# A convolution's intermediate values stored with another index first, and elementwise work moved from GpSimd to VectorE and ScalarE

## The chip, the cores and the metric

The kernel runs on one core of a Trainium2 chip. In the profile's names the core's engines are PE (TensorE: matrix products, with its weight loads as PEld), DVE (VectorE), ACT (ScalarE), POOL (GpSimd) and SP (SyncE, which here only issues DMAs). The metric is the device time of one execution in microseconds (us), given as the median of several runs.

## What is computed

Two layers of the same pair of blocks work on 2048 tokens of 512 channels, all in float32. The first block of a pair normalizes each token, convolves every channel along the tokens with a filter as long as the sequence, and adds the result. The second scores all tokens, sends the best two through a gated feed-forward network, and adds what comes out to those two tokens.

```python
P = exp((A * dt[:, None])[:, :, None] * pos)          # A: 512 x 128 complex, pos: 0..2047
K = 2.0 * einsum("dn,dnl->dl", C, P).real              # one filter per channel
y = irfft(rfft(u, 2 * L) * rfft(K, 2 * L))[..., :L]    # u: normalized x, by channel
x = x + (y + u * D_skip)
h = layernorm(x); r = h @ w_r; idx = argsort(-r)[:2]   # two tokens
x = x + h;  x[idx] += sigmoid(r[idx]) * ((silu(h[idx] @ w_gate) * (h[idx] @ w_up)) @ w_down)
```

The same filters serve both layers.

## The kernel before

The 512 channels are worked on in four blocks (`c` = 0 to 3) of 128. A block of x lies in a tile of 128 partitions with 16 tokens each. Each convolution is a transform in two steps, a product and the inverse in two steps, all made of small matrix products:

- `load`, `norm`: the block is loaded into `z`, and `affine` applies scale and shift, one of 16 slices at a time. Strings name the engine of each slice (A: ACT, G: POOL, V: DVE): in the second layer `NORM2` for blocks 1 to 3, `NORM0` for block 0.
- `f1a`, `f1b` (L815, L819): a product on PE, then a transpose on DVE, in eight parts, give the tile `g`, ordered by the first transform index.
- Then eight groups (`gi`). In the first layer's blocks 0 to 2: `kf_load`, `front_mm`, `front_tt` (p, L790), `back_mm` (pv, L801). In block 3 of the first layer and in all of the second: `group_kf` loads the filter's transform `kf` from DRAM, `group_mm` makes `pu` (L739), `group_tt` multiplies it with `kf` into `p` (DVE, L828, two buffers), and `group_y` forms the four parts of `y` (L843 a difference, L841 a sum; two buffers), each from one half of the partitions. They run on POOL, but for the last two groups of block 3, where the second half (`par` = 1) is DVE's. `i1_mm` turns `y` into `pv` (L849).
- `v_cp` (L1043) copies `pv` from PSUM on ACT. For blocks 0 to 2 the copy is a small tile `w` (two buffers), and `v_st` (L1046) stores it to DRAM in `vds`; once all eight are there, four loads (`v_ld`, `fin_load`, L872) bring the block back as `v` with another index on the partitions. `quad_mm` (po, L878) takes the last step on PE in four quarters, each with `d4`, and `quad_add` (L1058) adds it to x. Block 3 uses transposes on DVE (L860) in place of the trip through DRAM.
- Statistics and dot products for the next block follow on DVE (and a product on POOL), and `store` writes x. In the second layer `scale` applies the routed stage's normalization to x, one of 16 slices at a time, by the string `SCALE2`.

The DRAM tile `vds` has the shape 128 x 32 x 128: the partition of `pv` first (quarter g and 32 values b), then the 32 values k of the first transform index, then the channels. A store writes 2 KB for each partition. A load takes one quarter g: 32 partitions, one for each k, and for each of them 32 pieces of 512 bytes, so each load fills its 32 partitions for all b, and every quarter of po needs all four loads.

Beside the first layer's blocks 0 to 2, all engines also make the filters, in 32 steps (`KStep`: integer phases and decays on POOL, sines on ACT, products on DVE, contraction and transform on PE). The second layer has none of that.

The order of all this is written out by hand: the dictionary `PLAN` gives each operation of a lane (`t_y`, `t_vld`, ...) its place in one of five agendas: the first layer up to block 3; block 3 (`e_`); the routed stage (`r1`); the second layer (`t_`); the last routed stage (`r2`). `run` sorts an agenda and issues it, and `in_order` keeps each engine, SP's queue of DMAs included, in that order. An instruction that waits holds up all that stands behind it on its engine.

Of the kernel before, what the change touches and what calls it, by code (L numbers as in the profile page):

```python
# [32 lines left out]
    first=[7, 25],  # L33
    dt=[0, 1, 2, 3, 4, 5, 8, 10, 11, 12, 16, 18, 20, 24, 26, 27, 45, 51],
    setup=[
# [3 lines left out]
    ],  # L39
    setup2=[  # L40
# [3 lines left out]
    ],  # L44
    table=[191, 192, 193, 196, 197, 204, 205, 212, 220, 221, 223, 236, 237, 238, 239, 240, 243, 244, 246, 252, 253, 258, 259, 290],
    w=[101],
    x0=[21, 34, 91, 172],
    stat0=[
# [3 lines left out]
    ],  # L52
    params=[462, 484, 732, 784, 933, 1213],
    z=[261, 539, 841, 1189],
    norm=[
# [3 lines left out]
    ],  # L59
    f1a=[  # L60
        353, 402, 428, 451, 467, 490, 499, 521, 751, 772, 786, 788, 805, 812, 827, 839, 1004, 1087, 1097, 1102, 1121, 1126, 1136,
        1144, 1379, 1419, 1431, 1447, 1457, 1466, 1490, 1496,
    ],
    f1b=[
        370, 406, 446, 454, 472, 493, 519, 572, 766, 779, 787, 795, 806, 822, 831, 961, 1074, 1095, 1098, 1116, 1124, 1134, 1139,
        1166, 1409, 1423, 1436, 1449, 1465, 1475, 1493, 1524,
    ],
    kf_mm=[525, 530, 538, 560, 564, 566, 575, 579, 873, 901, 916, 918, 928, 929, 949, 950, 1207, 1218, 1226, 1227, 1245, 1252, 1253, 1273],
    kf_cp=[526, 548, 550, 561, 573, 574, 580, 585, 881, 902, 917, 926, 943, 946, 958, 973, 1219, 1223, 1231, 1232, 1251, 1254, 1268, 1276],
    kf_st=[553, 563, 594, 602, 934, 940, 966, 980, 1242, 1257, 1265, 1277],  # L70
    kf_load=[
        593, 615, 619, 649, 691, 692, 705, 748, 971, 981, 1005, 1006, 1007, 1048, 1062, 1079, 1263, 1288, 1305, 1325, 1341, 1369,
        1376, 1382,
    ],
    front_mm=[
        590, 604, 638, 661, 679, 702, 721, 749, 969, 991, 1008, 1026, 1034, 1055, 1063, 1069, 1286, 1306, 1324, 1336, 1340, 1363,
        1384, 1408,
    ],
    front_tt=[
        597, 624, 650, 674, 696, 708, 734, 758, 986, 996, 1018, 1032, 1045, 1057, 1065, 1085, 1299, 1307, 1328, 1337, 1349, 1371,  # L80
        1394, 1422,
    ],
# [28 lines left out]
    phase=[
# [7 lines left out]
    ],  # L119
    decay=[  # L120
# [9 lines left out]
    ],  # L130
    trig=[
# [5 lines left out]
    ],  # L137
    prod_b=[
# [238 lines left out]
def build(tc, x, lar, aim, cr, ci, ldt, dsk, wr, wg, wu, wd, d1_h, d1k_h, d4_h, w2_h, w3_h, w3b_h, sm_h, out):  # L377
# [6 lines left out]
    with ctx, in_order(tc, ORDER):  # L384
# [4 lines left out]
        def st(shape, nm, dt=F32, bufs=1):  # L389
            return cp.tile(shape, dt, name=nm, tag=nm, bufs=bufs)  # L390
# [1326 lines left out]
```

## Time and profile before

| | |
|---|---|
| median of 3 runs | 648.99 us (648.71 to 652.69) |
| the profiled execution | 647.57 us, span 645.7 us |
| mean granted clock of PE | 0.941 |
| HBM traffic | 82.82 MB read, 39.07 MB written |
| DMA packets | 83580, mean 190 GB/s |
| stores of w to `vds` | 48 of 256 KB, 4.0 us median to landing |
| loads of v from `vds` | 24 of 512 KB, 9.0 us median to landing |
| y on POOL | 152 of 160, some 0.73 us each |

The page gives the busy time of each engine with its share of the span. Busy time is no verdict on its own: an engine that is busy 70% of the span can be the bound in one stage and idle in another. Rows of groups read: line, engine, operation, output and inputs, count, then busy time and the mean of one in ns, then idle time just before and what ended it. Rows of waits read: who waited for whom, total us, times, and the longest. Rows of the timeline and of the chain begin with start and duration in us.

### The profile page before, as it was taken

Reading aid. Unit: us, or ns where it says so; the run is one execution under the profiler, and the core shown is the slowest. Engines: PE = TensorE matmul, PEld = TensorE weight load, DVE = VectorE, ACT = ScalarE, POOL = GpSimd, SP = SyncE. Lnnn points to the kernel's source line nnn. Section 1 sums busy time; section 2 is a strip of 40 time slices with the busy share of each in tenths; the row PEclk is TensorE's granted clock in tenths of the full one; section 3 lists DMA queues with packets and bytes.
Section 4 is the critical chain, followed back from the end, with each engine's and each line's share of the span. In section 5 each row is a group of like instructions: output and inputs, shape, how many; then the busy total and the mean of one; then the engine's idle time right before and its main releaser. Section 6 shows DMA issues by size and latency. Waiting matters only on the chain.

```text
span 645.7 us, 14016 instructions
## 1 busy us (share of the span) xinstructions
PE 459.8 (71%) x5316; PEld 348.4 (54%) x5316; DVE 461.7 (72%) x1004; ACT 326.2 (51%) x621; POOL 407.0 (63%) x630
## 2 busy tenths in 40 slices
PE   1002346778977689886986888777997998868846
PEld 0002334568864578656874675524786766664612
DVE  6997798757788656886886748735775679549941
ACT  3265847687957644678564323123365142142291
POOL 2489879788968334677362184360299889896280
PEclk9999986899999899999998999968999999889958
DMA  8736045887776768797758379964788999793962
GB/s 198 221 84 132 1 181 187 308 256 211 204 161 123 243 187 240 144 202 230 224 143 132 88 207 305 322 220 88 167 206 228 238 250 260 187 206 91 269 193 69
DMA packets 83580, 122.81 MB, mean 190 GB/s; under 512 B 6036, under 2 KB 61240, under 8 KB 79032
## 3 DMA queue, kind: packets, MB, share of 16 engines
q1 hardware_dynamic: 83384, 121.89, 71.2%
q8 instruction: 42, 0.69, 0.5%
q14 instruction: 26, 0.21, 0.1%
q0 software_dynamic: 128, 0.02, 0.0%
HBM read 82.82 MB, written 39.07 MB: 189 GB/s over the span
## 4 chain that ended last, share of the span: by engine, by line
DVE 22%; DMA 22%; PE 22%; POOL 14%; ACT 8%; issue 7%; SPq 4%; POOLq 0%; DVEq 0%; ACTq 0%
DMA kf<-kfd 4%; POOL y L843 4%; POOL y L841 4%; DMA kfd<-kd 4%; PE zf L815 4%; PE pv L801 4%; DMA v<-vd 4%; DMA vd<-w 3%; DVE sc L698 2%; DVE g L819 2%; PE po L878 2%; PE pv L849 2%; DMA b<-xs,b 2%; PE pg L1367 2%; DMA wgu<-in_wu 1%
## 5 line engine op out<-in xcount | busy, mean ns | idle before, releaser
L655 POOL TENSOR_TENSOR ph<-ph,pi 128x32 int32<-128x32 int32 (+4 forms) x160 | 88.0, 552 | 61.0 <-ACT ph L649 47.5
L667 POOL TENSOR_TENSOR mg<-mg,pf 128x32 f32<-128x32 f32 (+4 forms) x160 | 91.9, 574 | 32.1 <-ACT mg L660 25.3
L706 PE MATMUL pk<-sc 128*32 128x64 f32 x2048 | 39.6, 235 | 61.1 <-DVE rq0a L913 36.0
L698 DVE TENSOR_TENSOR sc<-tr,mg 128x1024 f32<-128x1024 f32 x64 | 76.8, 1209 | 5.3 <-ACT tr L683 3.6
L815 PE MATMUL zf<-z,d 128*128 128x256 f32 x256 | 74.6, 425 | 8.3 <-DVE g L819 5.3
L819 DVE STREAM_TRANSPOSE g<-zf 128x512 f32<-128x512 f32 x64 | 66.7, 1063 | 17.5 <-PE zf L815 16.3
L843 POOL TENSOR_TENSOR y<-p 64x256 f32<-64x256 f32 x76 | 55.2, 726 | 34.1 <-DVE p L828 27.4
L706 PEld LDWEIGHTS pk<-sc 128*32 128x32 f32 x2048 | 34.2, 120 | 72.0 <-ACT rq0b L911 36.3
L1043 ACT ACTIVATE w<-pv 128x512 f32<-128x512 f32 x48 | 28.4, 594 | 75.6 <-PE pv L849 26.8
L849 PE MATMUL pv<-y,w 128*128 128x128 f32 x320 | 51.4, 298 | 15.3 <-POOL y L841 15.1
L815 PEld LDWEIGHTS zf<-z,d 128*128 128x128 f32 x256 | 48.0, 205 | 23.5 <-DVE g L819 10.6
L828 DVE TENSOR_TENSOR p<-pu,kf 128x1024 f32<-128x1024 f32 x32 | 38.9, 1218 | 29.3 <-POOL y L841 21.3
L841 POOL TENSOR_TENSOR y<-p 64x256 f32<-64x256 f32 x76 | 55.1, 725 | 4.8
L849 PEld LDWEIGHTS pv<-y,w 128*128 128x128 f32 x320 | 42.4, 198 | 26.8 <-POOL y L841 21.3
L720 PE MATMUL kq<-d1k,kt 128*64 128x128 f32 x512 | 40.9, 309 | 22.4 <-DVE kt L713 20.7
L720 PEld LDWEIGHTS kq<-d1k,kt 128*64 128x64 f32 x512 | 32.1, 154 | 31.9 <-DVE kt L713 21.3
L730 ACT ACTIVATE gk<-kq 128x512 f32<-128x512 f32 x32 | 34.0, 1062 | 24.9 <-PE kq L720 23.4
L790 DVE TENSOR_TENSOR p<-pu,kf 128x1024 f32<-128x1024 f32 x24 | 29.2, 1218 | 22.7 <-DMA kf<-kfd 13.7
L739 PE MATMUL pu<-g,w 128*64 128x128 f32 x640 | 44.1, 287 | 1.5 <-DVE p L828 1.2
L739 PEld LDWEIGHTS pu<-g,w 128*64 128x64 f32 x640 | 36.9, 143 | 9.5 <-DVE p L828 3.5
L801 PE MATMUL pv<-p,w 128*128 128x128 f32 x192 | 38.4, 282 | 3.7 <-ACT w L1043 2.6
L801 PE MATMUL pv<-p,w3b 128*128 128x128 f32 x192 | 37.1, 275 | 0.0
(347 smaller groups left out, 1064.8 us busy)
## 6 DMA issues: line engine op xcount, KB each, us to landing
kf<-kfd SPq DMA_DIRECT2D x144, 128.0 KB, 3.7
vd<-w SPq DMA_DIRECT2D x48, 256.0 KB, 4.0
v<-vd SPq DMA_DIRECT2D x24, 512.0 KB, 9.0
kfd<-kd SPq DMA_DIRECT2D x16, 512.0 KB, 4.2
wd<-in_wd SPq DMA_DIRECT2D x4, 1792.0 KB, 17.1
x<-in_x SPq DMA_DIRECT2D x8, 512.0 KB, 7.0
w<-in_w SPq DMA_DIRECT2D x2, 2048.0 KB, 8.3
z<-in_x SPq DMA_DIRECT2D x8, 512.0 KB, 6.8
```

The costliest lines, as they stand in the source:

```text
L655: G.tensor_tensor(self.ph[:, :, n : 2 * n], self.ph[:, :, 0:n], self.step_of(self.pis, k + 1, n), op=OP.add)
L667: G.tensor_tensor(mg[:, :, 0:2, n : 2 * n], mg[:, :, 0:2, 0:n], by, op=OP.mult)
L698: V.tensor_tensor(sc.rearrange("p d (t i) -> p d t i", t=3)[:, :, 0:3:2, :], t, self.mg[:, :, 0:3:2, :], op=OP.mult)
L706: T.matmul(self.pk[32 * g : 32 * g + 32, e, :], t[:, 0:32], t[:, 32:96], start=k == 1, stop=k == 0, tile_position=(0, 32 * g))
L720: T.matmul(self.pq[64 * ri : 64 * ri + 64, e].rearrange("p g k -> p (g k)"), self.kt[:, e].rearrange("p h b -> p (h b)"), d1k[:, 128 * ri ...
L739: T.matmul(pt[64 * par : 64 * par + 64, ri, q, :], w2[:, k1, 64 * ri : 64 * ri + 64], src[:, k1, :], start=True, stop=True, tile_position= ...
L801: T.matmul(pv[:, k, :], w[:, j, :], p[t][:, k % 2, k // 2, :], start=t == 0, stop=t == 1)
L815: T.matmul(pf[:, 16 * s : 16 * s + 16, :], d1[:, 128 * s : 128 * s + 128], z[:, :, 16 * q : 16 * q + 16], start=True, stop=True)
L819: V.transpose(g[:, :, 16 * q : 16 * q + 16].rearrange("p k e -> p e k"), pf.rearrange("p b e -> p e b"))
L841: E.tensor_tensor(y[64:128, :, par, :], p[1][ls, 0], p[0][ls, 1], op=OP.add)
L843: E.tensor_tensor(y[0:64, :, par, :], p[0][ls, 0], p[1][ls, 1], op=OP.subtract)
L849: T.matmul(pv[:, k, :], w3[:, 4 * gi + k, :], y[:, k // 2, k % 2, :], start=True, stop=True)
```

## The change

It has three edits and a new order.

The DRAM tile `vds` becomes 32 x 128 x 128: k first, then the 128 partitions of `pv`, then channels. A store now writes, for each partition, four pieces of 512 bytes. A load takes eight values b of all 32 k and all four quarters g, with (k, g) as one index over the 128 partitions, and each partition receives one run of 4 KB. Loads 0 and 1 bring all that the first two quarters of po need, loads 2 and 3 the rest. Since the partitions of `v` are in another order now, `d4` gets a second copy with its rows permuted to match, used by `quad_mm`; `fin_mm` keeps the first.

In the second layer's blocks 0 to 2, one of the four parts of y in each group (the sum with `par` = 1) goes from POOL to DVE: 24 in all. `NORM2` and `SCALE2` become all A.

All lanes of `PLAN` are drawn anew; two of them stand below for their shape.

```diff
-    t_vld=[206, 215, 225, 230, 327, 328, 362, 364, 477, 481, 503, 508],
-    t_qm=[255, 271, 278, 303, 395, 431, 441, 448, 537, 539, 556, 561],
+    t_vld=[224, 228, 246, 280, 351, 367, 376, 430, 486, 491, 492, 499],
+    t_qm=[256, 259, 302, 323, 385, 389, 456, 461, 510, 526, 531, 558],
...
-NORM2 = "AAAAAAVAAAGGAAGA"
-SCALE2 = "VAAAAGAAAAAGAAAA"
+NORM2 = "AAAAAAAAAAAAAAAA"
+SCALE2 = "AAAAAAAAAAAAAAAA"
...
-        d4=d4.reshape(128, 64).astype(f),
+        d4=np.stack([d4.reshape(128, 64), d4.reshape(4, 32, 64).transpose(1, 0, 2).reshape(128, 64)], 1).astype(f),
...
-        d4 = st([128, 64], "d4")
+        d4 = st([128, 2, 64], "d4")
...
-        vds = [[dr.tile([128, 32, CH], F32, name=f"vd{i}_{c}", tag=f"vd{i}_{c}") for c in range(3)] for i in range(2)]
+        vds = [[dr.tile([32, 128, CH], F32, name=f"vd{i}_{c}", tag=f"vd{i}_{c}") for c in range(3)] for i in range(2)]
...
-            E = V if c == 3 and gi >= 6 and par else G
+            E = V if par and (c == 3 and gi >= 6 or c < 3 and layer and add) else G
...
-                T.matmul(po[64 * s : 64 * s + 64], d4, vt[:, 16 * s : 16 * s + 16, :], start=False, stop=True, tile_position=(0, 64 * s))
+                T.matmul(po[64 * s : 64 * s + 64], d4[:, 0], vt[:, 16 * s : 16 * s + 16, :], start=False, stop=True, tile_position=(0, 64 * s))
...
-            nc.sync.dma_start(vt[32 * g : 32 * g + 32], vds[layer][c][32 * g : 32 * g + 32].rearrange("b k e -> k b e"))
+            b0 = 16 * (g % 2) + 8 * (g // 2)
+            src = vds[layer][c].rearrange("k (g b) e -> (k g) b e", g=4)[:, b0 : b0 + 8, :]
+            nc.sync.dma_start(vt[:, b0 : b0 + 8, :], src)
...
-                T.matmul(po[64 * s : 64 * s + 64], d4, vt[:, b0 : b0 + 4, :], start=True, stop=True, tile_position=(0, 64 * s))
+                T.matmul(po[64 * s : 64 * s + 64], d4[:, 1], vt[:, b0 : b0 + 4, :], start=True, stop=True, tile_position=(0, 64 * s))
...
-                nc.sync.dma_start(vds[self.layer][self.c][:, 4 * i : 4 * i + 4, :], self.y.pop(("w", i)))
+                nc.sync.dma_start(vds[self.layer][self.c][4 * i : 4 * i + 4].rearrange("k p e -> p k e"), self.y.pop(("w", i)))
```

More of the change, by code (lines that the diff above doesn't have):

```diff
@@ L32 @@
 PLAN = dict(
-    first=[7, 25],
-    dt=[0, 1, 2, 3, 4, 5, 8, 10, 11, 12, 16, 18, 20, 24, 26, 27, 45, 51],
+    first=[11, 29],
+    dt=[0, 1, 2, 3, 5, 6, 7, 9, 10, 16, 18, 19, 20, 25, 26, 27, 35, 45],
     setup=[
[3 rows of a table removed]
[3 rows of a table added]
     ],
     setup2=[
[3 rows of a table removed]
-    ],
-    table=[191, 192, 193, 196, 197, 204, 205, 212, 220, 221, 223, 236, 237, 238, 239, 240, 243, 244, 246, 252, 253, 258, 259, 290],
-    w=[101],
-    x0=[21, 34, 91, 172],
[3 rows of a table added]
+    ],
+    table=[183, 204, 208, 209, 210, 211, 215, 223, 226, 229, 230, 235, 239, 240, 241, 242, 243, 245, 246, 252, 257, 260, 261, 267],
@@ L48 @@
+    w=[218],
+    x0=[17, 21, 113, 176],
     stat0=[
[3 rows of a table removed]
-    ],
-    params=[462, 484, 732, 784, 933, 1213],
-    z=[261, 539, 841, 1189],
[3 rows of a table added]
+    ],
+    params=[467, 525, 720, 782, 934, 1200],
+    z=[262, 559, 864, 1172],
     norm=[
[3 rows of a table removed]
[3 rows of a table added]
     ],
     f1a=[
-        353, 402, 428, 451, 467, 490, 499, 521, 751, 772, 786, 788, 805, 812, 827, 839, 1004, 1087, 1097, 1102, 1121, 1126, 1136,
-        1144, 1379, 1419, 1431, 1447, 1457, 1466, 1490, 1496,
+        357, 390, 443, 455, 472, 480, 491, 528, 752, 764, 771, 788, 801, 818, 829, 851, 1021, 1090, 1099, 1107, 1118, 1133, 1146,
+        1149, 1399, 1410, 1420, 1434, 1465, 1473, 1488, 1498,
@@ L77 @@
-        1384, 1408,
+        609, 617, 635, 658, 673, 708, 733, 749, 955, 996, 1018, 1024, 1043, 1062, 1070, 1075, 1277, 1287, 1305, 1324, 1346, 1365,
+        1374, 1405,
     ],
     front_tt=[
-        597, 624, 650, 674, 696, 708, 734, 758, 986, 996, 1018, 1032, 1045, 1057, 1065, 1085, 1299, 1307, 1328, 1337, 1349, 1371,
-        1394, 1422,
+        612, 631, 649, 668, 693, 723, 743, 760, 974, 999, 1020, 1035, 1045, 1063, 1072, 1082, 1283, 1303, 1314, 1336, 1355, 1367,
+        1384, 1411,
@@ L101 @@
+        1539, 1540, 1542, 1544, 1545,
     ],
-    store=[941, 1222, 1528],
+    store=[944, 1208, 1524],
     phase_0=[
-        137, 151, 218, 312, 329, 373, 392, 431, 473, 495, 522, 557, 598, 622, 663, 706, 738, 778, 843, 851, 911, 983, 1038, 1078,
-        1120, 1156, 1183, 1225, 1267, 1347, 1387, 1437,
+        136, 153, 202, 280, 335, 372, 398, 441, 469, 490, 524, 553, 582, 626, 664, 699, 765, 785, 822, 856, 921, 973, 1033, 1086,
+        1105, 1164, 1191, 1230, 1281, 1323, 1364, 1406,
     ],
@@ new lines @@
+    e_kmm=[1, 2, 4, 8, 12, 27, 28, 51],
+    e_kcp=[3, 5, 7, 10, 24, 36, 53, 63],
+    e_kst=[105, 119, 131, 164],
+    e_mm=[6, 11, 21, 22, 35, 45, 46, 60],
+    e_tt=[9, 15, 23, 29, 44, 56, 57, 74],
+    e_y=[14, 16, 17, 18, 19, 20, 25, 26, 32, 34, 37, 38, 39, 40, 41, 42, 48, 50, 52, 55, 59, 61, 65, 68, 69, 70, 72, 76, 78, 79, 80, 82],
+    e_i1=[30, 31, 47, 49, 64, 73, 77, 83],
+    e_v=[33, 43, 58, 62, 71, 75, 81, 84],
+    e_f0=[87, 67, 66, 54, 97, 88, 86, 117],
+    e_ft=[85, 89, 94, 96, 99, 106, 108, 114],
@@ L178 @@
+    e_fm=[90, 93, 95, 101, 102, 107, 121, 125],
+    e_fb=[98, 100, 103, 104, 115, 116, 123, 129],
+    e_w=[13, 91, 122, 134, 147, 149, 152, 160],
+    e_hm=[120, 127, 137, 156],
     e_hs=[
-        111, 115, 116, 129, 131, 132, 135, 136, 137, 138, 139, 140, 141, 145, 146, 147, 148, 149, 151, 153, 154, 155, 156, 157, 159,
-        160, 161, 162, 163, 164, 165, 167,
-    ],
-    e_hd=[123, 125, 158, 166],
-    e_st=[127],
+        109, 110, 111, 112, 118, 124, 126, 132, 133, 136, 138, 139, 140, 141, 142, 143, 144, 145, 146, 148, 150, 151, 153, 154, 155,
+        157, 158, 159, 161, 162, 163, 165,
+    ],
@@ L199 @@
+    r1_tab=[53, 59, 67, 71, 74, 81, 87, 99, 100],
+    r1_chg=[33, 69, 72, 75, 76, 83, 93, 94, 95, 96, 102, 103, 104, 105, 106, 137, 139, 141, 146],
+    r1_z=[47],
+    r1_n=[114, 115, 116, 117, 119, 120, 121, 122, 123, 124, 125, 126, 128, 129, 132, 133],
+    r1_fa=[142, 145, 150, 155, 160, 165, 168, 169],
+    r1_fb=[144, 147, 156, 162, 163, 166, 174, 175],
+    t_patch=[1, 2, 3, 4, 5, 6, 10, 20],
+    t_kf=[7, 8, 9, 17, 71, 105, 168, 210, 225, 282, 315, 348, 364, 388, 466, 478],
     t_mm=[
-        32, 37, 44, 45, 63, 98, 109, 123, 144, 156, 166, 181, 190, 218, 245, 251, 280, 287, 302, 316, 334, 361, 367, 401, 421, 427,
@@ L243 @@
+    t_f1a=[49, 50, 55, 64, 90, 97, 98, 112, 203, 204, 208, 213, 227, 232, 251, 252, 326, 330, 347, 352, 358, 363, 373, 391],
+    t_f1b=[51, 54, 85, 89, 94, 107, 117, 118, 205, 207, 216, 223, 237, 239, 260, 261, 335, 336, 354, 356, 366, 382, 405, 406],
+    t_f0=[546, 553, 560, 569, 577, 586, 581, 556],
+    t_hm=[585, 590, 642, 653],
     t_hs=[
-        580, 584, 589, 595, 601, 607, 608, 609, 610, 613, 614, 618, 621, 623, 624, 625, 629, 630, 635, 636, 638, 642, 643, 644, 645,
-        646, 648, 651, 652, 653, 654, 655,
+        579, 580, 583, 587, 588, 593, 594, 597, 602, 603, 605, 613, 615, 618, 623, 625, 626, 627, 628, 630, 631, 634, 636, 637, 638,
+        639, 640, 643, 646, 650, 656, 657,
@@ L282 @@
-    r2_w=[0, 1, 5, 6, 7, 8, 9, 10, 11, 12, 13, 14, 15, 16, 18, 19, 20, 21, 24, 25, 26, 27, 28, 29, 30, 31, 33, 55],
+        656, 659, 717, 742, 744, 756, 798, 809, 1008, 1022, 1064, 1065, 1080, 1081, 1097, 1108, 1317, 1331, 1350, 1379, 1380, 1425,
+        1441, 1442,
+    ],
+    v_ld=[814, 815, 816, 854, 1111, 1121, 1126, 1127, 1461, 1467, 1483, 1494],
+    quad_mm=[849, 852, 874, 886, 1162, 1173, 1187, 1192, 1490, 1499, 1504, 1521],
+    quad_add=[850, 855, 883, 887, 1163, 1182, 1188, 1196, 1495, 1502, 1509, 1522],
@@ new lines @@
+    t_vst=[93, 95, 111, 128, 144, 150, 195, 196, 221, 222, 238, 254, 265, 300, 311, 340, 350, 371, 372, 380, 403, 422, 444, 460],
+    t_vld=[224, 228, 246, 280, 351, 367, 376, 430, 486, 491, 492, 499],
+    t_qm=[256, 259, 302, 323, 385, 389, 456, 461, 510, 526, 531, 558],
+    t_qa=[262, 293, 319, 383, 395, 445, 504, 517, 527, 528, 541, 563],
+    t_dm=[287, 359, 412, 413, 452, 470, 518, 522, 559, 582, 596, 629],
+    t_ds=[337, 379, 424, 459, 501, 521, 534, 548, 567, 595, 619, 648],
+    t_ft=[554, 555, 565, 572, 573, 592, 600, 601],
@@ L283 @@
+    t_fm=[557, 561, 568, 575, 584, 599, 608, 617],
+    t_fb=[564, 566, 574, 576, 589, 607, 616, 621],
+    e_wd=[92, 113],
+    t_wd=[570, 571],
+    r1_w=[0, 1, 2, 3, 4, 5, 6, 7, 8, 9, 10, 11, 12, 13, 15, 22, 23, 24, 29, 31, 34, 40, 49, 73, 78, 79, 84, 118],
+    r2_w=[0, 1, 2, 3, 4, 5, 6, 7, 8, 9, 10, 11, 12, 13, 14, 15, 16, 18, 19, 31, 42, 45, 47, 51, 53, 54, 55, 57],
 )
```

140 lines of the change are left out of this document (50 added, 90 removed), and 109 rows, old and new, of tables (decay, norm, out, phase).

## The prediction

> **What bounds the kernel now.** I read the page's shares, its slices and the chain that ended last, cut the span into stages with the table of windows, and asked for waits and groups inside the stage that the change touches most.
>
> ```profile
> PE 459.8 (71%) x5316; PEld 348.4 (54%) x5316; DVE 461.7 (72%) x1004; ACT 326.2 (51%) x621; POOL 407.0 (63%) x630
> DVE 22%; DMA 22%; PE 22%; POOL 14%; ACT 8%; issue 7%; SPq 4%; POOLq 0%; DVEq 0%; ACTq 0%
> ```
> Over the whole span no engine stands out, and the chain is shared between DVE, DMA and PE. So the answer must come from stages.
>
> ```profile
> core 0: us, PE busy (x) PEld busy (x) DVE busy (x) ACT busy (x) POOL busy (x), PEclk, DMA share, GB/s
> 465.40:582.50 117.10, 100.39 (x855) 79.12 (x856) 77.60 (x105) 48.06 (x110) 103.57 (x144) 0.96 0.94 222
> 465.40:545.00 79.60, 71.33 (x616) 56.29 (x616) 55.45 (x66) 36.15 (x85) 70.05 (x99) 1.00 0.97 233
> 339.60:366.80 27.20, 19.86 (x351) 13.07 (x349) 19.95 (x67) 11.03 (x14) 4.09 (x5) 0.94 0.61 109
> 0.00:367.00 367.00, 234.35 (x3590) 190.17 (x3592) 282.19 (x568) 226.71 (x376) 232.73 (x393) 0.96 0.67 179
> ```
> The first row is the second layer's convolution, from its first y to its last. POOL is busy 103.57 of 117.10 us there with 144 instructions. The chain shows what lies between two of them:
>
> ```profile
> 465.36 0.74 POOL y L843
> 466.10 0.07 issue
> 466.16 0.73 POOL y L841
> ```
> A gap of 0.07 us after each of 144 makes 10.1 us more, 113.7 of 117.1 together (97%). The waits of the same stretch say the same from the other side:
>
> ```profile
> ACT w L1043 <- DMA vd<-w: 23.2, 8, 4.6
> DVE p L828 <- POOL y L841: 21.3, 13, 3.0
> PE pv L849 <- POOL y L841: 12.6, 13, 2.4
> DVE g L819 <- PE zf L815: 4.3, 8, 0.9
> POOL y L843 <- DVE p L828: 3.2, 3, 1.7
> POOL y L843 <- DMA kf<-kfd: 1.5, 1, 1.5
> ```
> POOL waits 4.7 us in all; DVE and PE wait for POOL. This stretch is bound by POOL. Just behind come PE (100.39 us, 86%) and the DMA engines (share 0.94). The first layer (0 to 367 us) has no such engine: DVE is busiest with 282.19 of 367, so order and latency decide there.
>
> The other place is the loads of v, four of 512 KB for each of three blocks and two layers.
>
> ```profile
> 183.63 2.02 DMA vd<-w
> 187.40 12.25 DMA v<-vd
> 339.64 12.32 DMA v<-vd
> 352.01 1.98 PE po L878 x4
> ```
> Twice in the first layer the chain runs through the four loads and then into po.
>
> **The change part by part.**
>
> *1. POOL gives up y and normalizations.*
>
> ```profile
> L841 POOL TENSOR_TENSOR y<-p 64x256 f32<-64x256 f32 x62 | 44.8, 723 | 4.0
> L810 POOL TENSOR_SCALAR z<-z,b 128x128 f32<-128x128 f32 x9 | 4.1, 456 | 20.1 <-DVE g L1554 19.8
> L810 POOL TENSOR_SCALAR x<-x,b,b 128x128 f32<-128x128 f32 x4 | 1.8, 460 | 0.3
> L810 POOL TENSOR_SCALAR xw<-xw,b,b 128x128 f32<-128x128 f32 x4 | 1.8, 448 | 0.4
> L808 ACT ACTIVATE xw<-xw,b,b 128x128 f32<-128x128 f32 x26 | 11.3, 482 | 0.0
> 462.89 1.41 POOL L810 TENSOR_SCALAR z<-z,b 128x128 f32<-128x128 f32 x3 [19.82 <-DVE g L1554]
> 464.28 0.44 POOL L810 TENSOR_SCALAR x<-x,b,b 128x128 f32<-128x128 f32 x1
> ```
> One y in four of blocks 0 to 2 leaves: 24 x (0.723 + 0.07) = 19.0 us. Of the 17 normalizations four (the last two rows) lie ahead of the stretch; 13 x (0.45 + 0.07) = 6.8 us leave it. POOL's need falls from 113.7 to 88 us. ACT gets these and five from DVE, at most 22 x 0.482 = 10.6 us, on 48.06 of 117.10; I cost that at nothing, since ACT mostly waits there (23.2 us for stores alone). If that cover were gone it would cost those 10.6.
>
> *2. What a y costs on DVE.* Eight of them run there already, in block 3:
>
> ```profile
> L841 DVE TENSOR_TENSOR y<-p 64x256 f32<-64x256 f32 x4 | 3.4, 850 | 0.1
> L843 DVE TENSOR_TENSOR y<-p 64x256 f32<-64x256 f32 x4 | 3.2, 798 | 0.6 <-PE pv L849 0.5
> 386.61 0.81 POOL L841 TENSOR_TENSOR y<-p 64x256 f32<-64x256 f32 x1
> ...
> 388.27 0.72 POOL L841 TENSOR_TENSOR y<-p 64x256 f32<-64x256 f32 x1
> 388.71 0.57 DVE L841 TENSOR_TENSOR y<-p 64x256 f32<-64x256 f32 x1
> ...
> 583.27 1.34 POOL L1063 TENSOR_TENSOR m<-xw,wrt 128x512 f32<-128x512 f32 x1
> 583.49 1.40 DVE L841 TENSOR_TENSOR y<-p 64x256 f32<-64x256 f32 x1
> ```
> They take 0.82 us on average (6.6 / 8), from 0.49 to 1.40, and the last four rows (from the timeline) show why: POOL's operation ends at 388.99 and the DVE one at 389.28; the other pair ends at 584.61 and 584.89. Both times DVE ends 0.28 us after POOL, however early it began. So a y on DVE is 0.28 us of work and the rest of whatever POOL is doing. [...] I take 0.82: 24 x 0.82 = 19.7 us, bounds 24 x 0.28 = 6.7 and 24 x 1.40 = 33.6. POOL loses a little too: the one y that ran into a DVE one (the row of 386.61) took 0.81 against 0.72, so 24 x 0.09 = 2 us, and it needs 90. DVE has 77.6 + 19.7 less some 2 us of normalizations, 95. Queued behind the y in DVE's order are the next p and the transposes g; PE's pu and zf need their buffers.
>
> Now the needs are POOL 90, DVE 95, PE 100, in a stretch of 117.1. The gain lies between 0 (the order finds no room) and 16.7 us (PE full). With three engines above 90 us in each other's chains I take about a third: **6 us**.
>
> *3. The loads of v.* Before, a load fills 32 partitions in 512-byte pieces (1024 for 512 KB); after, 128 partitions with 4 KB each (128 pieces). The DMA view, first from 187 to 200 us, where the loads are nearly alone, then from 183 to 186.2 us, 0.08 us a slice, with one store of 256 KB in 2 KB pieces alone:
>
> ```profile
> DMA packets 4089, 2.25 MB, mean 173 GB/s; under 512 B 64, under 2 KB 4066, under 8 KB 4066
> GB/s 0 0 0 0 0 0 0 0 0 0 0 0 0 0 0 0 0 0 179 384 410 384 410 410 384 358 282 77 0 0 0 0 0 0 0 0 0 0 0 0
> PE po L878 <- DMA v<-vd: 3.2, 2, 2.0
> DVE xc L1058 <- PE po L878: 4.9, 3, 4.3
> ```
> Small pieces run at 173 GB/s, so 2 MB take 12 us; large ones reach 384 to 410, and 2 MB at that rate are 5.3 us. Moreover the first two quads need only the first two loads now. So po can begin some 7 us earlier. What is that worth? PE stood still for v only 3.2 us in the whole run (row over the full span). But at the end of the first layer, 339.6 to 366.8 (row above), DVE is busy 19.95 of 27.20 us, 4.9 us of its idle time waits for po (row from 339 to 368 us), and behind xc stand the dot products and statistics that keep DVE until the p of block 3 at 366.84. At best DVE's idle 7.2 us goes. I take 4 there and 1 at 199.7: **5 us**, bounds 0 and 9. What is late next is the last filter block, whose transforms run in the same 12 us. In the second layer no wait for v is listed.
>
> *4. The stores of v* pay: 512 pieces of 512 bytes for 256 KB, where 128 of 2 KB were. The row above gives 0.7 us for a store today; at the rate of the small-piece loads it is 1.5. That is 48 x 0.8 = 38 us more DMA time, against 24 x 1.7 = 41 us less on loads (512 KB at 173 and at 384 GB/s): DMA work is moved, not removed. A later landing holds the two buffers of w, for which ACT waits above; ACT has room for 8 waits x 0.8 = 6.4 us, and if it had not, that is the cost. I take **+0.5 us**, bounds 0 and 6.4. [...] No run here shows a 512-byte store; the sum goes by the loads' rate.
>
> *5. The order.* Every lane of the plan is drawn anew. In SP's queue the same weight loads still stand ahead of the store that closes block 3, and the routed stage keeps its chain, so I put 0 on it. No row prices a redrawn order; my estimate of the spread is 6 us either way, the size of DVE's idle time at the handover above.
>
> **Sum**: -6 - 5 + 0.5 = -10.5 us. The profiled execution took 647.57 us (span 645.7 and 1.87 around it), so 637.1; the median of the runs, 648.99, lies 1.42 above the profiled one: **638.5 us**.
>
> **Rivals.**
>
> *DVE takes over what POOL gives up* (27 in 100). From 465.4 to 545 us, where all 24 y would lie, DVE is busy 55.45 of 79.60. With 19.7 more it is 75, and the 4.3 us that it waits for zf are PE's: nothing is left to gain. [...] Against it: with POOL less busy a y meets it less often. Then part 1 brings 0 to 2 us, and the time is 647.57 - 4.5 + 1.42 = 644.5, within 1%.
>
> *The written pieces choke the DMA engines* (15 in 100, with a DVE y well over 1 us in it). In the stretch the share is 0.94, so 7 us are spare; its 12 loads of v free 12 x 1.7 = 20. Its 24 stores may then take 27 / 24 = 1.1 us more than 0.7: from 1.8 us for a store, which is 57 ns for a piece on one of 16 engines against 48 ns for a read piece (12.25 us x 16 / 4096), DMA is the bound. At 75 ns a piece a store takes 2.4 us, 24 x 1.7 - 27 = 14 us are lost, and even with the 5 us of the first layer the time is 658: slower. For it: SP issues all in order, so kf loads queue behind. Against it: nothing in the trace says that writing a piece costs more than reading one.
>
> *The loads keep small pieces*, so that the change doesn't do what it says: part 3 then brings nothing and the time is 643.5. The new view gives each partition one run of 4 KB, so I hold this for nearly excluded and count it with the first rival.
>
> **How the numbers follow.** About 1% is what a measurement of this kernel can tell from no change, so faster means under 642.5 and slower over 655.5. The forecast and what lies below it have 58 in 100. With part 1 at 16.7 and part 3 at 9 the time is 624; I leave the last of that out and start the range at 626. Upward it takes in the first rival and reaches to 655, leaving out most of the second.
>
> **What would show it.** Right: packets fall to about 80500 (24 loads with 896 fewer, 48 stores with 384 more, from 83580 on the page), and the four loads take 5 to 7 us; POOL's adds drop by 24 and DVE's y rise to 32 in all, at 0.5 to 0.9 us each; the stretch of y shrinks to about 111 us with PE near 90%; no wait of DVE for po over 2 us at the handover. Wrong: DVE above 90% in that stretch with y above 1 us; landings of vd well over 5 us with ACT's wait for them above 30; or a routed stage that starts later because the redrawn order moved its weights.

## Result, and the profile after

The changed kernel takes 627.44 us in the median (four runs, 625.84 to 631.94), the kernel before beside it 648.85 (four runs). The ratio is 0.968 with a 95% interval of 0.962 to 0.973: 21.4 us less, where 10.4 were forecast. The time lies inside the range, at its lower end. The profiled execution took 625.84 us with a span of 623.9.

The first row is the page's busy times after; then a row of the DMA issues (count, KB each, median us to landing), and the windows that answer to those shown of before: the stretch of y in the second layer (first y to the last operation of the last), the handover at the end of the first layer, and the first layer. The columns are the same as in the prediction.

```profile
PE 455.3 (73%) x5316; PEld 346.3 (56%) x5316; DVE 477.5 (77%) x1021; ACT 335.0 (54%) x645; POOL 383.3 (61%) x589
v<-vd SPq DMA_DIRECT2D x24, 512.0 KB, 5.1
448.36:562.76 114.40, 100.48 (x872) 78.47 (x872) 94.58 (x126) 57.25 (x135) 86.25 (x109) 0.99 0.84 229
324.00:351.00 27.00, 23.23 (x450) 16.43 (x450) 25.02 (x80) 14.09 (x19) 5.78 (x8) 1.00 0.60 165
0.00:351.00 351.00, 230.75 (x3590) 190.58 (x3592) 280.86 (x568) 226.80 (x376) 231.62 (x393) 0.96 0.65 188
```

The loads land in 5.1 us where they took 9.0. (Both are medians of the loads whose landing the profile tells: 11 of 24 here, but before only 6 of 24, all in the second layer. A comparison of like with like follows in the experiments.) In the stretch of y POOL falls from 105.64 (row below) to 86.25 us and DVE rises from 80.00 to 94.58. In the first layer the engines have hardly less to do than before (DVE 280.86 against 282.19 us, PE 230.75 against 234.35), but they have it done 16 us sooner: at the handover, where DVE was busy 19.95 of 27.20 us, it is now busy 25.02 of 27.00.

The stretch of before by the same ends, the first quarter of po, and the first y of block 3 (the end of the first layer's blocks 0 to 2), in the windows and the timeline of before; then that first y after:

```profile
465.36:584.89 119.53, 102.82 (x866) 80.78 (x868) 80.00 (x107) 48.69 (x111) 105.64 (x145) 0.96 0.92 218
199.70 1.08 PE L878 MATMUL po<-v,d 128*64 128x512 f32 x4 [1.97 <-DMA v<-vd]
368.12 0.72 POOL L843 TENSOR_TENSOR y<-p 64x256 f32<-64x256 f32 x1 [24.19 <-DVE p L828]
```
```profile
352.31 0.73 POOL L842 TENSOR_TENSOR y<-p 64x256 f32<-64x256 f32 x1 [22.06 <-DVE p L827]
```

So 15.8 of the 21.8 us by which the span shrank (645.7 to 623.9) were gained before block 3 begins, and 5.1 in the stretch of y (119.53 to 114.40). The rest, 0.9, lies in block 3, the routed stages and the tail. In the stretch of y, the waits of after:

```profile
POOL y L842 <- DVE p L827: 32.9, 8, 20.8
ACT w L1044 <- PE pv L848: 23.6, 11, 4.7
ACT w L1044 <- DMA vd<-w: 12.7, 3, 6.4
DVE p L827 <- POOL y L840: 7.1, 4, 3.0
PEld pv L848 <- POOL y L840: 6.8, 9, 1.3
DVE g L818 <- PE zf L814: 5.1, 4, 2.2
```

DVE waits for POOL 7.1 us (was 21.3), and it is POOL that waits now: 12.1 us inside the stretch (32.9 less the 20.8 that lie ahead of its first y). PE, at 100.48 of 114.40 (88%), is the fullest engine. Of the signs that the prediction named, the packets came out as foreseen (80508, where about 80500 were expected), and at the handover DVE waits for po 0.9 us in all. The first layer is the surprise, and most experiments are about it.

### The profile page after: what moved, and what is told of

Read it like the earlier page. It is cut to its first block, busy times and chain, and to the rows that moved or that the text cites. A ratio compares the mean times of both kernels' runs of the same rounds, so it can differ in the third digit from the quotient of the medians.

```text
span 623.9 us, 14032 instructions
## 1 busy us (share of the span) xinstructions
PE 455.3 (73%) x5316; PEld 346.3 (56%) x5316; DVE 477.5 (77%) x1021; ACT 335.0 (54%) x645; POOL 383.3 (61%) x589
## 2 busy tenths in 40 slices
DMA packets 80508, 122.83 MB, mean 197 GB/s; under 512 B 5909, under 2 KB 61241, under 8 KB 75961
## 5 line engine op out<-in xcount | busy, mean ns | idle before, releaser
L666 POOL TENSOR_TENSOR mg<-mg,pf 128x32 f32<-128x32 f32 (+4 forms) x160 | 89.6, 560 | 41.3 <-ACT mg L659 34.2
L842 POOL TENSOR_TENSOR y<-p 64x256 f32<-64x256 f32 x76 | 57.5, 757 | 69.3 <-DVE p L827 55.0
L814 PE MATMUL zf<-z,d 128*128 128x256 f32 x256 | 71.9, 412 | 10.1 <-DVE g L818 8.1
L814 PEld LDWEIGHTS zf<-z,d 128*128 128x128 f32 x256 | 46.0, 198 | 25.7 <-DVE g L818 16.4
L848 PE MATMUL pv<-y,w 128*128 128x128 f32 x320 | 47.9, 290 | 12.4 <-POOL y L840 6.6
L848 PEld LDWEIGHTS pv<-y,w 128*128 128x128 f32 x320 | 40.6, 193 | 22.1 <-POOL y L840 10.3
L719 PE MATMUL kq<-d1k,kt 128*64 128x128 f32 x512 | 39.3, 302 | 17.6 <-DVE kt L712 17.6
L719 PEld LDWEIGHTS kq<-d1k,kt 128*64 128x64 f32 x512 | 31.0, 150 | 26.6 <-DVE kt L712 21.8
L738 PE MATMUL pu<-g,w 128*64 128x128 f32 x640 | 42.7, 280 | 3.8 <-DVE p L827 3.2
L679 ACT ACTIVATE tr<-ph 128x1024 f32<-128x1024 int32 x32 | 33.1, 1035 | 15.6 <-POOL ph L654 7.4
L840 POOL TENSOR_TENSOR y<-p 64x256 f32<-64x256 f32 x52 | 37.9, 728 | 3.2
```

Of the source, the lines that this page charges most:

```text
L666: G.tensor_tensor(mg[:, :, 0:2, n : 2 * n], mg[:, :, 0:2, 0:n], by, op=OP.mult)
L719: T.matmul(self.pq[64 * ri : 64 * ri + 64, e].rearrange("p g k -> p (g k)"), self.kt[:, e].rearrange("p h b -> p (h b)"), d1k[:, 128 * ri ...
L738: T.matmul(pt[64 * par : 64 * par + 64, ri, q, :], w2[:, k1, 64 * ri : 64 * ri + 64], src[:, k1, :], start=True, stop=True, tile_position= ...
L814: T.matmul(pf[:, 16 * s : 16 * s + 16, :], d1[:, 128 * s : 128 * s + 128], z[:, :, 16 * q : 16 * q + 16], start=True, stop=True)
L840: E.tensor_tensor(y[64:128, :, par, :], p[1][ls, 0], p[0][ls, 1], op=OP.add)
L842: E.tensor_tensor(y[0:64, :, par, :], p[0][ls, 0], p[1][ls, 1], op=OP.subtract)
```

## The experiments

All runs in one table. "First y" is when block 3 of the first layer begins, "stretch" the time from the first y of the second layer to the end of the last, both from each run's profile. The last column is the ratio to the kernel before, measured beside it, with its 95% interval. Eight profiles with the redrawn first agenda and loads that bring half of v first put the first y at 349.1 to 355.7 us, so a difference under some 6 us in this column is not read from one profile. In the second column the four profiles with the redrawn order, the early half and a quarter of y on DVE lie between 113.3 and 115.4 us.

| run | first y | stretch | ratio |
|---|---|---|---|
| kernel before | 368.1 | 119.5 | 1 |
| changed kernel | 352.3 | 114.4 | 0.968 (0.962 to 0.973) |
| layout_only | 364.5 | 118.5 | 0.991 (0.988 to 0.994) |
| order_only | 377.2 | 132.0 | 1.030 (1.023 to 1.037) |
| all_but_layout | 378.8 | 130.1 | 1.025 (1.017 to 1.033) |
| layout_order | 352.9 | 119.4 | 0.972 (0.963 to 0.981) |
| first_new | 349.1 | 119.1 | 0.973 (0.968 to 0.979) |
| early_new | 361.1 | 120.6 | 0.986 (0.981 to 0.992) |
| late_new | 360.7 | 120.7 | 0.981 (0.975 to 0.987) |
| four_loads | 368.2 | 128.1 | 1.011 (1.003 to 1.018) |
| small_pieces | 351.7 | 113.3 | 0.967 (0.962 to 0.971) |
| last_first | 361.1 | 119.2 | 0.985 (0.979 to 0.990) |
| old_last_first | 365.1 | 119.6 | 0.991 (0.988 to 0.994) |
| quarter_loads | 354.8 | 114.5 | 0.966 (0.960 to 0.972) |
| first_new_eng | 353.1 | 124.3 | 0.979 (0.972 to 0.986) |
| first_new_y | 355.7 | 119.8 | 0.974 (0.968 to 0.980) |
| no_strings | 354.1 | 115.4 | 0.965 (0.959 to 0.971) |
| half_y | 352.9 | 121.6 | 0.981 (0.975 to 0.986) |

### Which part of the change gains

Four runs take the change apart. `layout_only` is the kernel before with the new DRAM tile, its loads, stores and second `d4`. `layout_order` adds the redrawn `PLAN`:

```diff
 # layout_order, against the changed kernel
-            E = V if par and (c == 3 and gi >= 6 or c < 3 and layer and add) else G
+            E = V if c == 3 and gi >= 6 and par else G
-NORM2 = "AAAAAAAAAAAAAAAA"
-SCALE2 = "AAAAAAAAAAAAAAAA"
+NORM2 = "AAAAAAVAAAGGAAGA"
+SCALE2 = "VAAAAGAAAAAGAAAA"
```

`order_only` is the kernel before with the redrawn `PLAN`, `all_but_layout` the same with the engine edits. In the old layout every quarter needs all four loads, so in these two the fourth load stands ahead of the first quarter:

```diff
-    v_ld=[814, 815, 816, 854, 1111, 1121, 1126, 1127, 1461, 1467, 1483, 1494],
+    v_ld=[814, 815, 816, 848.5, 1111, 1121, 1126, 1127, 1461, 1467, 1483, 1489.5],
-    t_vld=[224, 228, 246, 280, 351, 367, 376, 430, 486, 491, 492, 499],
+    t_vld=[224, 228, 246, 255.5, 351, 367, 376, 384.5, 486, 491, 492, 499],
```

> The kernel before with the new layout of vds alone (stores, loads, d4); old order, old engines. T1 (the prediction's terms: loads worth 5 us at the end of the first layer only, stores 0.5): 644 us, and the first layer's block 3 starts its y 4 to 5 us earlier than 368.1. T2 (each of the first layer's three boundaries between blocks has the loads on its path, so the layout alone gives the 16 us of that layer): 633 us, block 3 starts near 353. T3 (the redrawn order gave the first layer's gain): 648 us, block 3 near 368.

> The kernel before with the redrawn order alone; old layout and old engines. Three loads of v are moved ahead of the first quarter of po, which the old layout needs. T1 and T2: within 3 us of before, 646 to 652. T3: block 3's y starts near 353, and the time is 633.

> The changed kernel with the old layout (same three loads moved). T1: the engines' 6 us remain, 643. T2: 643, with block 3's y at 368 or later. T3: 628, as the changed kernel.

> The changed kernel with y and the normalizations on their old engines. T1: 644 (the layout's 5 us). T2: 633, the second layer's stretch of y back at some 119 us. T3: 633 too, so it only tells T1 from the others and prices the engine edits in the new order at the difference to 627.4.

Measured: layout alone 645.85 us, 0.991; order alone 669.97, 1.030; order and engines 666.36, 1.025; layout and order 632.49, 0.972. None of the three theories holds. The layout alone gives about what the prediction's terms for it said (0.9% of 650 us is 5.7, where 5 less 0.5 were forecast), the order alone costs 3%, and both together gain 2.8%. The reason why the order alone loses is in its waits:

```profile
DVE xc L1057 <- PE po L877: 30.5, 10, 9.8
PE po L877 <- DMA v<-vd: 24.8, 5, 8.9
DVE xc L1058 <- PE po L878: 7.2, 7, 4.3
```

(The third row is the kernel before.) With slow loads PE stands still for v 24.8 us (3.2 in the kernel before): the redrawn order reaches the quarters before the loads have landed, and DVE waits behind PE, 30.5 us where it was 7.2. The same order with the new loads, in `layout_order` and in the changed kernel, lists no wait of PE for v at all.

### Where in the order the gain lies

The order of one agenda can be cut at a label and continued in another's order. `first_new` takes the redrawn first agenda and leaves all later ones old; `early_new` the redrawn first agenda up to the first load of v and the old order from there; `late_new` the complement, with the later agendas redrawn. All have the new layout and the old engines.

```python
# the rule for early_new (late_new has the two orders exchanged);
# in the kernel's text it stands as new numbers for the lanes
pre = new[: new.index(("v_ld", 0))]
first = pre + [w for w in old if w not in pre]
```

> The new layout, the engines as before, the redrawn order for the first agenda alone (the first layer up to block 3); all later agendas in the old order. Both orders so far gave, with the new layout, 645.85 (old) and 632.5 us (new), a ratio of 0.9912 and 0.9717 to the kernel before. By the traces 11.6 of these 13.4 us lie ahead of the first y of block 3 (364.5 and 352.9 us). If the first agenda is the place, 645.85 - 11.6 = 634.3 us, ratio 0.974, first y of block 3 near 353. If the later agendas carry the gain, near 645, ratio 0.99.

> The new layout, engines as before. In the first agenda all operations that the redrawn order has ahead of the first load of v come in that order, the rest in the old order; later agendas old. Theory H (the handovers: the redrawn order gains from the loads on, since the quarter products stand sooner behind them in PE's queue): the part ahead of the loads is worth at most 1 us, so 645 us, first po near 198. Theory P (packing: the redrawn order has brought PE two or three transforms further by the time the loads are issued, and the quarters come sooner for that): first po near 192 to 194, 6 us gained, 640 us.

> The complement: in the first agenda everything ahead of the first load of v in the old order, all behind it in the redrawn one, the later agendas redrawn too; new layout, engines as before. Theory H: nearly all of the gain stays, 633 to 635 us, first po near 193. Theory P: the transforms that the old order had not yet done still stand ahead of the first quarter, first po 196 to 198; the 6 us of the first handover are lost and the rest (7 us) stays, near 639 us.

Measured: first_new 631.3 us, 0.973, with the whole gain of layout_order, so the first agenda is the place. early_new 641.67, 0.986; late_new 638.26, 0.981. Against layout_only (0.991) the part ahead of the first load brings 0.5% and the part from there on 1.0%, as theory P had it within 2 us, first quarters included (194.5 and 197.8 us). Theory H falls: it had 645 us for early_new and 633 to 635 for late_new. The two parts are less sure than their sum, for the intervals of early_new and layout_only overlap. PE's timeline behind the first loads shows how they combine. layout_only first (its four loads are issued at 186.87), then the changed kernel (185.87); PE's work on the filters in between is left out:

```profile
186.87 1.76 SPq L874 DMA_DIRECT2D v<-vd  x4
188.13 1.13 PE L815 MATMUL zf<-z,d 128*128 128x256 f32 x4
190.77 1.13 PE L815 MATMUL zf<-z,d 128*128 128x256 f32 x4 [0.47 <-DVE g L819]
195.10 1.13 PE L815 MATMUL zf<-z,d 128*128 128x256 f32 x4
197.42 1.13 PE L815 MATMUL zf<-z,d 128*128 128x256 f32 x4 [0.17 <-DVE g L819]
198.48 1.08 PE L880 MATMUL po<-v,d 128*64 128x512 f32 x4
```
```profile
185.87 1.76 SPq L873 DMA_DIRECT2D v<-vd  x4
188.72 1.13 PE L814 MATMUL zf<-z,d 128*128 128x256 f32 x4
191.35 1.13 PE L814 MATMUL zf<-z,d 128*128 128x256 f32 x4 [0.28 <-DVE g L818]
193.34 1.03 PE L879 MATMUL po<-v,d 128*64 128x512 f32 x4
194.29 1.13 PE L814 MATMUL zf<-z,d 128*128 128x256 f32 x4
195.35 1.08 PE L879 MATMUL po<-v,d 128*64 128x512 f32 x4
```

Both issue the loads at the same place, but behind them the old order still has four transforms ahead of the first quarter and the redrawn one two: one more was done earlier, and one comes between the quarters. The first quarter starts 7.5 us after the issue, not 11.6.

### What makes the loads early enough

`four_loads` keeps the new tile and the redrawn order but lets each load fill 32 partitions, in pieces of 16 KB; `small_pieces` keeps 128 partitions but pads each row of the tile to 1 KB, so that pieces are 512 bytes; `last_first` changes only the order of the four loads. four_loads and last_first issue the fourth load ahead of the first quarter; four_loads has the old engines, the others the new.

```diff
 # four_loads
+            src = vds[layer][c].rearrange("k (g b) e -> (k g) b e", g=4)
+            nc.sync.dma_start(vt[32 * g : 32 * g + 32], src[32 * g : 32 * g + 32])
 # small_pieces (stores and loads take [..., :CH])
-        vds = [[dr.tile([32, 128, CH], ...
+        vds = [[dr.tile([32, 128, 2 * CH], ...
 # last_first
-            b0 = 16 * (g % 2) + 8 * (g // 2)
+            b0 = 16 * (g % 2) + 8 * (1 - g // 2)
```

> The redrawn order and the new DRAM tile, engines as before (as in the run with layout and order, 632.5 us), but each load fills 32 partitions in pieces of 16 KB rather than 128 partitions in pieces of 4 KB, so that every quarter of po needs all four loads; the fourth load is issued ahead of the first quarter. If it is enough that pieces are large: landings of 5 to 6 us and 633 us. If it matters that half of the loads bring the first two quarters: the first po begins 2 to 3 us later at each of three handovers, 638 to 641 us. If 32 partitions take the data at half the rate (landings near 9 us again): as with the old layout in this order, 655 to 670 us.

> The changed kernel with each row of the DRAM tile padded from 512 to 1024 bytes (half of it unused): the stores write the same 512-byte pieces, and a load still fills 128 partitions but reads 1024 pieces of 512 bytes, as the kernel before did over 32 partitions. Two theories of why the loads became fast (landing 9.0 to 5.1 us, the rate 173 to some 400 GB/s). Size of the pieces, as the prediction has it: landings are near 9 us again, PE waits some 25 us for v as in the redrawn order with the old layout, 655 to 668 us. Number of partitions, for which the run with 16 KB pieces over 32 partitions speaks (7.8 us, 656 us): landings stay at 5 to 6 us and the time at 627 to 630.

> The changed kernel with the four loads in the other order, so that the first two quarters of po need the third and fourth load; all four are issued ahead of the first quarter. Pieces and partitions are unchanged. If it matters that half of the loads bring the first quarters, po waits for the rest of the 5 to 6 us that four loads take: 2 to 3 us at each of the first layer's three handovers, 633 to 636 us. If the rate alone matters: 627 to 629 us.

Measured: four_loads 656.05 us, 1.011, slower than the kernel before; small_pieces 627.55, 0.967, the same as the changed kernel; last_first 639.38, 0.985, 12 us more (6 to 9 were expected). The DMA view from 186 to 200 us, 0.35 us a slice: the changed kernel, then small_pieces, then four_loads.

```profile
DMA packets 681, 2.84 MB, mean 203 GB/s; under 512 B 80, under 2 KB 80, under 8 KB 592
GB/s 0 0 140 246 281 246 293 375 375 410 445 269 246 386 386 398 421 410 375 211 70 47 12 0 0 0 0 0 47 0 187 187 164 211 281 257 211 94 141 304
```
```profile
DMA packets 4101, 3.06 MB, mean 219 GB/s; under 512 B 91, under 2 KB 3972, under 8 KB 3972
GB/s 233 332 348 382 298 276 285 291 293 293 300 297 281 272 265 266 274 310 239 101 51 19 19 0 47 23 328 117 211 304 304 211 164 258 304 211 257 117 140 23
```
```profile
DMA packets 728, 2.38 MB, mean 170 GB/s; under 512 B 81, under 2 KB 599, under 8 KB 599
GB/s 6 3 22 285 278 398 421 234 421 94 47 421 281 0 281 328 140 47 375 234 94 281 328 140 47 421 187 94 140 375 234 0 94 47 0 0 0 0 0 0
199.47 1.98 PE L878 MATMUL po<-v,d 128*64 128x512 f32 x4 [3.33 <-DMA v<-vd]
```

Pieces of 512 bytes into 128 partitions ran at 265 to 310 GB/s in 14 slices on end of small_pieces' row (173 on average into 32, in the kernel before). The 4 KB pieces reach 445 in single slices; their 2 MB fill 18 slices, 6.3 us, some 330 GB/s on average by an estimate from that row. This last step is worth nothing in the time. Pieces of 16 KB into 32 partitions come in bursts with gaps and fill 31 slices, 10.9 us, about as long as the 512-byte pieces of before; the first quarter waits for them until 199.47, and PE, idle for 3.33 us, begins the transform that stands behind it at 201.38.

The medians of all loads (9.0, 7.8, 6.6 and 5.1 us for the kernel before, four_loads, small_pieces and the changed kernel) don't compare like with like, since the order differs too: order_only has the loads of before and a median of 7.6. The next rows are for the first layer alone and for one order, the redrawn one: order_only, four_loads, small_pieces, the changed kernel. Each tells of four to six of the twelve loads, the first two of a handover, and the longest is in each the second load of a handover.

```profile
DMA to landing us min/median/max: 4.8/6.4/8.6
DMA to landing us min/median/max: 5.6/6.9/8.1
DMA to landing us min/median/max: 4.1/5.9/6.6
DMA to landing us min/median/max: 3.7/4.2/5.5
```

Into 32 partitions the longest took 8.6 us in pieces of 512 bytes and 8.1 in pieces of 16 KB; into 128 partitions 6.6 and, in pieces of 4 KB, 5.5. So the partitions shortened the loads more than the pieces did: the smallest pieces into 128 partitions beat the largest into 32. The table tells the same. With all four loads needed ahead of the first quarter, order_only (32 partitions, 512 bytes) has 1.030, four_loads (32, 16 KB) 1.011, and last_first (128, 4 KB) 0.985, of which the engine edits account for some 0.4%; the early half then brings 0.968. Larger pieces came with 2% less time where 32 partitions kept the loads slow (from order_only to four_loads, where the pieces of the stores shrank too, from 2 KB to 512 bytes), and with none where 128 partitions had made the loads fast enough (from small_pieces to the changed kernel). Two things remain open. The distance between a partition's pieces in DRAM changed along with the partitions (16 KB in the old tile, 1 KB in small_pieces), and part of four_loads' gaps may come from its few pieces, 32 to a load; no run tells these apart.

Why loads into 32 partitions take longer was not shown. In single slices theirs reached 421 GB/s too (four_loads); on average they moved 173 GB/s before, and 2 MB took 10.9 us in four_loads.

last_first shows the other half: pieces, partitions and rate are those of the changed kernel, but the first quarter needs the last load. At the third handover it stands still for it, and its products take 3.21 us where 1.08 are usual:

```profile
343.17 3.21 PE L879 MATMUL po<-v,d 128*64 128x512 f32 x4 [2.53 <-DMA v<-vd]
```

At the first handover this wait is some 1 us, at the second there is none, and in the whole run PE stands still for v 6.0 us. How these grow to 12 us behind PE is open. The first y comes at 361.1 us, and the stretch of y takes 119.2: the second layer gains from the early half too.

### Why the old order gains so little, and whether more is left

`old_last_first` makes the same exchange of loads in layout_only. `quarter_loads` goes further in the changed kernel: load g brings exactly what quarter g needs.

```diff
 # quarter_loads
+            src = vds[layer][c].rearrange("k (g s b) e -> (k g) s b e", g=4, s=2)[:, :, 4 * g : 4 * g + 4, :]
+            nc.sync.dma_start(vt.rearrange("p (s b) e -> p s b e", s=2)[:, :, 4 * g : 4 * g + 4, :], src)
```

> The new layout in the old order with the old engines (645.85 us and 0.9912 in its run), but with the four loads in the other order, so that the first two quarters of po need the third and fourth load. In the redrawn order this cost 12 us. Theory S (slack: the old order reaches the first quarter 11 to 12 us after the loads are issued, when all four have long landed, so it can use neither the half nor the rate beyond what it got): 645 to 647 us, ratio 0.99. Theory U (the old order lives on the half of the loads too): 650 to 658 us, ratio 1.00 to 1.01.

> The changed kernel with each load bringing exactly one quarter of what po needs (two pieces of 2 KB for each of 128 partitions in place of one of 4 KB), so that the first quarter of po needs only the first load and the second only the second. If the wait for v still costs something in the changed kernel: 2 to 5 us less, 622 to 625 us, a version faster than both. If, as its waits say (none of PE for v), the first half is early enough: 626 to 628 us.

Measured: 644.82 us, 0.991, the same ratio as layout_only: in the old order the early half is worth nothing. PE reaches the first quarter 11 to 13 us after the loads are issued in the first layer, and neither run lists a wait of PE for v. Theory S holds. quarter_loads: 627.47, 0.966, the same as the changed kernel. PE has no wait for v in either, and a still earlier first quarter of v gains nothing in this order.

### The engine edits

`no_strings` is the changed kernel with the old `NORM2` and `SCALE2`. `first_new_eng` and `first_new_y` are first_new with both engine edits, and with y on DVE alone: the later agendas in the old order. `half_y` doubles the y given to DVE.

```diff
 # half_y
-            E = V if par and (c == 3 and gi >= 6 or c < 3 and layer and add) else G
+            E = V if par and (c == 3 and gi >= 6 or c < 3 and layer) else G
```

> The changed kernel with the normalizations of the second layer back on their old engines (y on DVE stays). The two engine edits together bring 5 us in this order (stretch of y 119.4 to 114.4 us). If y on DVE brings it alone: 114 to 115 us for the stretch, 627 to 628 us, 0.967. If the normalizations bring a share by their part of what POOL is relieved of (6.8 of 25.8 us): 116 us, 629 us, 0.969. If all of it: 119 us, 632 us, 0.972.

> The changed kernel (new layout, y on DVE and normalizations on ACT) with the later agendas, block 3 and the second layer among them, in the old order; the first agenda stays redrawn. Without the two engine edits this order gave 0.9733 of the kernel before, about as much as the fully redrawn one (0.9717). If the engine edits are worth their 5 us by themselves: 0.966, 626 to 628 us, the same as the changed kernel. If the redrawn later order is what makes room for y on DVE: about 631 us, no gain over the run without the edits.

> The first agenda redrawn, the later ones in the old order, new layout, y on DVE as in the change, but the normalizations on their old engines. With both engine edits the stretch of y in the second layer took 124.3 us in this order (637.5 us, 0.9789), without them 119.1 (631 us, 0.9733). If y on DVE is what the old order has no room for: again about 124 us, 0.979. If the normalizations, all on ACT, were at fault: 119 us or less, 0.973.

> The changed kernel with both parts of y of the second half (48 of the 96 of the second layer's blocks 0 to 2) on DVE where it has 24. In the stretch of y DVE is busy 94.75 of 114.6 us and POOL 86.25; 24 more at 0.57 us (the median so far) take DVE to 108 and POOL to 68. Theory D (DVE takes over from there, the rival of the prediction): the stretch grows by 4 to 10 us, 632 to 638 us. Theory E (the order, not an engine's sum, bounds the stretch): within 2 us of the changed kernel, 626 to 629 us.

Measured: no_strings 627.49 us, 0.965, stretch 115.4; first_new_eng 637.49, 0.979, 124.3; first_new_y 633.45, 0.974, 119.8; half_y 635.95, 0.981, 121.6. In the redrawn order y on DVE brings 4.0 of the 5.0 us from layout_order, and the normalizations at most 1, which is no more than such profiles differ by. In the whole time the two edits are not clear of noise: layout_order has 0.972 (0.963 to 0.981), the changed kernel 0.968. In the old later order the same y brings nothing (119.1 without, 119.8 with), with 94.75 us of DVE and 90.14 of POOL in the stretch, the sums that gain in the redrawn order:

```profile
451.86:571.62 119.76, 100.43 (x859) 80.29 (x860) 94.75 (x131) 48.13 (x110) 90.14 (x121) 0.95 0.81 218
449.51:573.83 124.32, 104.06 (x860) 83.56 (x860) 92.37 (x126) 56.68 (x133) 84.38 (x108) 0.90 0.78 210
```
```profile
449.12:564.55 115.43, 99.68 (x870) 76.59 (x870) 96.19 (x132) 48.92 (x112) 92.80 (x124) 1.00 0.83 226
```

(first_new_y, first_new_eng; then no_strings.) Why both edits together come out longer in the old order stays open: the granted clock was 0.90 in that profile and PE was busy 3.6 us more than in first_new_y, and the intervals of the two ratios overlap.

In half_y the next row is the stretch, then its y on DVE:

```profile
449.44:571.00 121.56, 99.87 (x870) 77.49 (x870) 107.98 (x151) 57.55 (x135) 69.32 (x84) 0.99 0.78 215
L840 DVE TENSOR_TENSOR y<-p 64x256 f32<-64x256 f32 x28 | 19.5, 698 | 0.5
L842 DVE TENSOR_TENSOR y<-p 64x256 f32<-64x256 f32 x28 | 14.8, 530 | 1.1 <-PE pv L848 0.3
```

Twenty-four more y put DVE at 107.98 of 121.56 us, 89%, with POOL at 57%, and the stretch is longer than without any y on DVE (119.4). Theory D holds: a quarter of y is a gain, half a loss. No run was measurably faster than the changed kernel.

## Why the prediction was wrong, step by step

*The order was put at nothing; this is the step that failed.* The prediction has "so I put 0 on it", with 6 us either way. With the new loads the order is worth 0.991 to 0.972, 12 to 13 us; with the old loads it costs 3%. I had judged it by itself, by its weights and its chain, while its worth lies in what it does with the other edits: it brings the quarters to PE soon after half of v has landed (at the first handover 7.5 us after the issue, where the second load took 5.5).

*The loads, worth 5 us (0 to 9): right for the old order, too small for the new.* Alone they gave 5.7. The price came from the waits for v, 3.2 us of PE, and from the idle DVE of one handover. Those rows show what a load costs an order that was drawn around slow loads and had filled their time with transforms; what can be won by a shorter one does not appear as a wait. The first quarter came 6.4 us earlier already at the first handover (199.7 to 193.3), where 1 us was allowed, and the first y of block 3 came 15.8 us earlier, where 5 were.

*The rate: right in size, wrong in cause.* The prediction let 2 MB land in 5.3 us by the rate of a store in 2 KB pieces; 6.3 were measured. It took larger pieces to be the cause. The runs show that the partitions shortened the loads more, and that 512-byte pieces into 128 of them give the same time (small_pieces). "the first two quads need only the first two loads now" was a half-sentence in the prediction; last_first prices it at 12 us, more than the whole forecast.

*POOL, DVE and y: right in size, in part by luck.* 6 us were forecast and 5.1 came in the stretch; DVE was to have 95 us and has 94.58. The terms were off in ways that cancel: a y on DVE takes less than the 0.82 us that I took, 21.0 / 32 = 0.66, and the gain needs the redrawn order. The forecast of 6 was a third of what was possible, taken without a row that gives it.

```profile
L840 DVE TENSOR_TENSOR y<-p 64x256 f32<-64x256 f32 x28 | 18.3, 655 | 0.8
L842 DVE TENSOR_TENSOR y<-p 64x256 f32<-64x256 f32 x4 | 2.7, 675 | 0.4 <-PE pv L848 0.3
L840 DVE TENSOR_TENSOR y<-p x28: 417/572/1476, 373.0 to 561.4; 64x256 f32<-64x256 f32 x28
561.15 1.33 POOL L1064 TENSOR_TENSOR m<-xw,wrt 128x512 f32<-128x512 f32 x1
561.37 1.39 DVE L840 TENSOR_TENSOR y<-p 64x256 f32<-64x256 f32 x1
```

The last two rows show what the prediction read from two pairs of before: POOL's product ends at 562.48, DVE's y 0.28 us behind it, at 562.76. But half of the y of line L840 took 0.57 us or less (the third row: fastest, median, slowest in ns). The fastest took 0.42, so the 0.28 us that the prediction called the work of a y, and with it the lower bound of 6.7 us, was too little. And POOL paid as well as DVE: its y of line L842 took 0.757 us on average, where those of before took 0.726, some 2.4 us over 76 of them, near the 2 us that were allowed. The normalizations cost ACT nothing that shows and gave at most 1 us.

*The stores, +0.5 us: nothing speaks against it.* No run prices the stores alone. The fastest store of 512-byte pieces landed after 2.3 us, the fastest 2 KB one after 2.0:

```profile
DMA to landing us min/median/max: 2.0/4.0/9.0
```
```profile
DMA to landing us min/median/max: 2.3/4.0/8.6
```

The medians are equal, and ACT's wait for stores fell (12.7 us in the stretch, 23.2 before). That agrees better with a term near 0 than with the loads' rate, by which a store would take 1.5 us and not 0.7.

*The rivals.* DVE takes over only at twice the y (half_y). The written pieces did not choke the DMA engines: their share in the stretch fell from 0.92 to 0.84. The loads did as the change says.

## What to carry to other kernels

A shorter transfer and the order around it are one edit: measured apart, one gave 1% and the other lost 3%; together they gained 3%. The waits of a tuned kernel price a transfer only for the order that was drawn around it, so when both change, ask what the new order puts right behind the landing, and how much of the data it needs there. In this kernel it paid to cut a load so that its first part serves the first consumer (0.968, and 0.985 in last_first), and to spread it over all partitions before making its pieces larger (the longest load of the first layer took 6.6 us where it took 8.6; larger pieces into 32 partitions brought 8.1).

## What the runs showed of the hardware

The same 2 MB took 10.9 us into 32 partitions for each load even in pieces of 16 KB, while pieces of 512 bytes into 128 partitions ran at 265 to 310 GB/s in 14 slices on end (four_loads and small_pieces). SyncE's time to issue the four loads changed too: 4.29 us in the kernel before, 2.65 in four_loads, 1.76 in the changed kernel, and 4.96 in small_pieces. So 1024 pieces to a load were the dearest whether they went into 32 or 128 partitions; why 32 large pieces took longer than 128 smaller ones is open.

```profile
185.78 4.29 SPq L872 DMA_DIRECT2D v<-vd  x4
```
```profile
186.51 2.65 SPq L872 DMA_DIRECT2D v<-vd  x4
184.22 4.96 SPq L873 DMA_DIRECT2D v<-vd  x4
```
